# GpSimd's residuals wait for more of VectorE's instructions: the sign subtractions and the low parts of V

## The chip, the cores and the metric

The kernel runs on one core of a Trainium2 chip. Its time is the device time of one execution in microseconds (us). The profile names the engines PE (TensorE, matmuls), PEld (TensorE's loading of weights), DVE (VectorE), ACT (ScalarE), POOL (GpSimd) and SP (SyncE, which issues transfers).

## The reference

Two stages follow each other. The first is attention for 4 batches of 8 heads, 768 tokens, 64 columns, in which a query sees only the keys of its own hash bucket (the signs of six projections). The second lets each batch choose its 128 best tokens and adds a two-layer network's output to them.

```
mask = q_bucket[:, :, :, None] == k_bucket[:, :, None, :]
scores = np.where(mask, scale * q @ k.T, -1e9)
attn = softmax(scores);  x = attn @ v                       # float32, heads side by side
top = the 128 tokens of a batch with the largest x @ w_gate
out[top] = x[top] + sigmoid(score) * (relu(x[top] @ w1) @ w2)
```

## The kernel before, in words

Float32 values are carried as sums of two 16-bit parts, so that TensorE can work on 16-bit operands. For each of the 32 heads (h) the kernel

- places the head's queries, keys and hash signs as columns of a tile A (and low parts in B), by transfers from SyncE's queue;
- takes the row maxima of the masked scores (`max_unit`, L646, on TensorE; L654 on ScalarE; L663 on VectorE);
- computes the scores transposed, in nine units of 512 columns (`st_unit`, L697 and L701), and their exponentials P in float32 on ScalarE (`st_exp`, L715 and L717). P of a head comes in three tiles of two chunks each, P{h}_0 to P{h}_2;
- subtracts from P its upper 16 bits and so gets the residual R{h}_g of each tile (`r_chunk`): on VectorE one chunk at a time (L732), or on GpSimd both chunks at once (L735). `POOL_R` gives GpSimd tile 1 of the even heads and tiles 0 and 2 of the odd ones, none of the last head: 46 residuals;
- multiplies on TensorE (`av`, L760), per chunk and block of 128 queries, the upper half of P with V's high and low part, and R with V's high part, in this order. TensorE takes its matmuls in the order of the program.

V of a pair of heads is split into a high part by ScalarE (L550) and a low part by VectorE (`split_vl`, L556); for the last head the column of scores also has a low part (`score_vl`, L578). The signs of a group of four heads (two pairs) are made by `signs`: two comparisons on VectorE (L482) after the hash matmuls (L465), and, after the second half, the difference of the two halves of the keys' signs (L489; group 0's is on GpSimd). `k_diff` makes the same difference of the keys (L636). GpSimd also makes the low halves of the network's weights (`load_w`, L821), 16 subtractions.

The order of the work on all engines is written out by hand: ORDER is a list of event numbers, which the program issues one after the other; a negative number resumes a generator. One stretch of it (line 119) reads

```
45, 1300, 1208, 1277, 1153, 1043, 44, 46, -1, 1099, 1285, 1100, 1221, 1103, 1301, 1104, 1105,
```

where 44 and 46 are the two halves of `signs` for group 4, 1100 and 1103 are `r_chunk` of head 13 for the tiles 0 and 2 (R13_0 and R13_2, on GpSimd), 1104 and 1105 the first of head 13's products. A few numbers further on stands 1101, VectorE's residual R13_1.

Beside the waits for data, two helpers add waits by order. `mine(i)` notes a VectorE instruction as the latest one, and `turn(i)` makes a GpSimd subtraction wait until the VectorE instruction noted last is done. Before the change `mine` stands around L502 (low parts of queries and keys), L565, L636, L732 and L843 (comparisons for the ranks); `turn` stands around L735 and L821, 62 instructions.

Of the kernel before, what the change touches and what calls it, by code (L numbers as in the profile page):

```python
# [16 lines left out]
ALU = mybir.AluOpType  # L17
# [224 lines left out]
def body(ctx, tc, qk, v, pj, wg, w1, w2, cst, out):  # L242
    nc = tc.nc
# [113 lines left out]
    def mine(i):  # L357
        st["port"] = i
# [9 lines left out]
    def need(*keys):  # L368

        assert all(k in st for k in keys), keys  # L370
# [101 lines left out]
    def signs(g, e):  # L472
        hp = st["hp", g, e]
        if ("sg", g) not in st:
            st["sg", g] = sb.tile([P, S // 2 + S], F16, tag="sg", name=f"sg{g}", bufs=2)
        if g > 1:
            need(("ps", 4 * g - 4))
        for j in range(2):
            st["sgd", 2 * g + j, e] = True
        t = st["sg", g]  # L480
        sd, sg = t[:, : S // 2], t[:, S // 2 :]
        nc.vector.tensor_scalar(  # L482
            sg[:, e * 384 : (e + 1) * 384], hp[:, :384], pjt[:, 66:67], pjt[:, 67:68],
            op0=ALU.is_gt, op1=ALU.mult,
        )
        pmax.give(f"hp{g}_{e}")
        if e:
            eng = nc.vector if g else nc.gpsimd
            eng.tensor_tensor(sd, sg[:, 0:384], sg[:, 384:768], op=ALU.subtract)  # L489

    def split_xh(p, r):
        if ("T", p) not in st:
# [59 lines left out]
    def split_vl(pr):  # L552
        need(("vh", pr))
        st["vl", pr] = True
        t, vv = st["V", pr], V[pr % NV].rearrange("p c h d -> p (c h) d")
        nc.vector.scalar_tensor_tensor(  # L556
            vv[:, :, VL : VL + D], t.rearrange("p c h d -> p (c h) d"), VS, vv[:, :, :D],
            op0=ALU.mult, op1=ALU.subtract,
        )

    def score_v():
        need(("vh", NH // 2 - 1))
# [12 lines left out]

    def score_vl():
        need("gvh")
        nc.vector.scalar_tensor_tensor(  # L578
            V[VLAST][:, :, 1, VL + D + 1 : VL + OW], st["gv"], VS, V[VLAST][:, :, 1, D + 1 : OW],
            op0=ALU.mult, op1=ALU.subtract,  # L580
        )
        st["gvl"] = True

    def sum_v(g):
# [642 lines left out]
    for g in range(NH // 4):  # L1227
        for e in range(2):
            at(hash_half, g, e)
            at(signs, g, e)  # L1230
    for fn in (score_v, score_vh, score_vl):
        at(fn)
# [4 lines left out]
    for h in range(NH):  # L1237
# [15 lines left out]
        if h % 2 == 0:  # L1253
            for fn in (load_v, split_vh, split_vl):
                at(fn, h // 2)
            g, k = GROUP[h // 2]
            if k == len(SUMS[g]) - 1:
                for fn in (sum_v, sum_hi, sum_lo):
                    at(fn, g)
# [92 lines left out]
```

## Time and profile before

| | |
|---|---|
| median of 3 runs | 392.65 us (392.45 to 396.61) |
| the profiled execution's own time | 393.02 us |
| its span, first to last instruction | 391.2 us |
| busy: PE, PEld, DVE, ACT, POOL | 379.8, 276.0, 326.1, 333.4, 180.2 us |
| chain that ended last, share on PE | 81% |
| L735 on POOL, 46 instructions | 132.3 us busy, 2879 ns mean, 138.4 us idle before them |
| L556 on DVE, 16 instructions | 15.4 us busy, 961 ns mean |
| L489 on DVE, 7 instructions | 2.5 us busy, 358 ns mean |

Times of instructions count from the span's start. The difference of 1.8 us between the execution's time and its span lies outside of all instructions. A row of a timeline gives the start, the duration, engine, line and operation, what it writes and reads, and in brackets how long its engine had been idle before it, with what ended that.

### The profile page before, as it was taken

What the parts mean: (1) busy time and instruction counts of PE and PEld (TensorE: products, weight loads), DVE (VectorE), ACT (ScalarE), POOL (GpSimd) and SP (SyncE); (2) the same over time, 40 slices, a digit from 0 to 9 for tenths busy, and PEclk for the clock granted to TensorE, in tenths of its full rate; (3) what the DMA queues carried; (4) which work ended last, traced back from release to release, by engine and by line L of the source; (5) the groups of instructions that cost most, each with busy time, mean ns of one, the idle gap of its engine ahead of it and who ended that gap; (6) DMA issues with size and microseconds to landing.
All of it is one profiled execution on the core that took longest, in us unless ns stands there. A gap on an engine that the chain in (4) does not pass through costs nothing.

```text
span 391.2 us, 14365 instructions
## 1 busy us (share of the span) xinstructions
PE 379.8 (97%) x5768; PEld 276.0 (71%) x5768; DVE 326.1 (83%) x903; ACT 333.4 (85%) x817; POOL 180.2 (46%) x103
## 2 busy tenths in 40 slices
PE   7889999999999999999999999999999999999995
PEld 4247677677766777787757777677777778778794
DVE  4879888889899989888897889988998888689732
ACT  6989999999999999988879999989999897775310
POOL 6436676564647268652245343555335354500122
PEclk9999999999999999999999999999999999999999
DMA  8676676677566377375583536646654422000511
GB/s 266 151 198 193 168 235 180 198 218 209 147 189 179 95 186 208 103 211 144 144 238 104 131 85 165 160 112 153 195 155 111 94 55 66 22 22 2 175 45 54
DMA packets 26354, 56.38 MB, mean 144 GB/s; under 512 B 4218, under 2 KB 10942, under 8 KB 26288
## 3 DMA queue, kind: packets, MB, share of 16 engines
q1 hardware_dynamic: 15936, 36.92, 36.0%
q10 hardware_dynamic: 9680, 16.45, 13.2%
q0 software_dynamic: 672, 2.10, 1.7%
q8 instruction: 45, 0.74, 0.8%
q14 instruction: 21, 0.17, 0.1%
HBM read 26.58 MB, written 7.35 MB: 87 GB/s over the span
## 4 chain that ended last, share of the span: by engine, by line
PE 81%; ACT 7%; issue 4%; DMA 4%; POOL 1%; DVE 1%; SPq 1%; POOLq 0%; ACTq 0%
PE av L760 25%; PE st L697 14%; PE st L701 14%; PE bank L646 14%; PE bank L978 4%; PE bank L465 3%; PE bank L1002 3%; DMA A<-sg 2%; ACT me L654 2%; ACT P L715 2%; PE av L745 1%; ACT x L784 1%; DMA out_3l_dram<-x 1%; ACT P L717 1%; DMA Xa<-in_qk_dram 1%
## 5 line engine op out<-in xcount | busy, mean ns | idle before, releaser
L735 POOL TENSOR_TENSOR R<-P 128x1536 f16<-128x1536 f32 x46 | 132.3, 2879 | 138.4 <-ACT P L717 25.1
L760 PEld LDWEIGHTS <-P 128*128 128x128 bf16 x2304 | 125.5, 98 | 25.4 <-issue 1.1
L760 PE MATMUL av<-V,P 128*128 128x65 f16 (+2 forms) x2304 | 132.5, 193 | 0.0
L663 DVE CUSTOM_DVE_ANT_0 mj<-bank,me 128x384 bf16<-128x384 f32 x192 | 102.2, 552 | 29.6 <-ACT me L654 14.5
L760 PE MATMUL av<-V,R 128*128 128x65 f16 (+1 forms) x1152 | 125.8, 193 | 0.0
L715 ACT ACTIVATE P<-st 128x512 f32<-128x512 f32 x192 | 113.8, 613 | 10.4 <-PE st L701 4.3
L697 PE MATMUL st<-A 128*128 128x512 f16 (+1 forms) x384 | 119.1, 326 | 0.2
L701 PE MATMUL st<-B 128*128 128x512 f16 (+1 forms) x384 | 118.7, 325 | 0.0
L646 PE MATMUL bank<-A 128*128 128x384 f16 x384 | 107.5, 331 | 4.9 <-DMA A<-sg 2.7
L760 PEld LDWEIGHTS <-R 128*128 128x128 f16 x1152 | 105.8, 97 | 0.1
L654 ACT ACTIVATE me<-bank 128x384 f32<-128x384 f32 x192 | 94.3, 510 | 10.7 <-DVE M L663 4.8
L732 DVE TENSOR_TENSOR R<-P 128x768 f16<-128x768 f32 x100 | 94.9, 964 | 0.3 <-ACT P L717 0.2
L717 ACT ACTIVATE P<-st 128x512 f32<-128x512 f32 x96 | 58.8, 613 | 2.4 <-PE st L701 2.0
L646 PEld LDWEIGHTS <-A 128*128 128x128 f16 x384 | 35.3, 98 | 26.9 <-issue 6.8
L701 PEld LDWEIGHTS <-B 128*128 128x128 f16 x384 | 37.5, 98 | 15.4 <-issue 1.2
L697 PEld LDWEIGHTS <-A 128*128 128x128 f16 x384 | 37.5, 98 | 15.2 <-issue 2.5
L784 ACT ACTIVATE x<-av,rc 128x64 f32<-128x64 f32 x192 | 44.3, 334 | 0.4 <-DVE rc L772 0.4
L502 DVE SCALAR_TENSOR_TENSOR T<-X,T 128x768 f16<-128x768 f32 x32 | 30.9, 971 | 0.0
L495 ACT ACTIVATE T<-X 128x768 f16<-128x768 f32 x32 | 27.7, 867 | 0.0
L978 PEld LDWEIGHTS <-w1h 128*128 128x128 f16 x256 | 15.9, 98 | 2.6
L821 POOL TENSOR_TENSOR w1l<-W,w1h 128x512 bf16<-128x512 f32 x8 | 12.9, 1616 | 8.0 <-DVE R L732 7.8
L821 POOL TENSOR_TENSOR w2l<-W,w2h 128x512 bf16<-128x512 f32 x8 | 12.5, 1562 | 8.6 <-PE bank L646 3.7
(138 smaller groups left out, 405.0 us busy)
## 6 DMA issues: line engine op xcount, KB each, us to landing
X<-in_qk_dram SPq DMA_DIRECT2D x32, 384.0 KB
B<-T SPq DMA_DIRECT2D x62, 192.0 KB
A<-T SPq DMA_DIRECT2D x31, 240.0 KB
V<-in_v_dram ACTq DMA_DIRECT2D x16, 384.0 KB
out_dram<-x ACTq DMA_DIRECT2D x6, 768.0 KB
W<-in_w_dram ACTq DMA_DIRECT2D x8, 512.0 KB
sbc<-scores SPq DMA_DIRECT2D x3, 384.0 KB
A<-sg SPq DMA_DIRECT2D x31, 31.5 KB
```

What stands on the lines that cost most here:

```text
L646: nc.tensor.matmul(pt[:, :384], a[0][:, t * P : (t + 1) * P], a[1][:, 384:768] if i else K[h % NA], start=True, stop=True,)
L654: nc.scalar.activation(me, st["mx", h, t, 0][:, :384], AF.Relu)
L663: nc.vector.tensor_tensor_reduce(out=jk, in0=st["mx", h, t, 1][:, :384], in1=st["me", h, t], op0=ALU.add, op1=ALU.max, scale=1.0 / MS, sca ...
L697: nc.tensor.matmul(pt[:, o : o + n], a[1][:, c * P : (c + 1) * P], a[0][:, q0 : q0 + n], start=True, stop=False,)
L701: nc.tensor.matmul(pt[:, o : o + n], bt[:, 0, c * P : (c + 1) * P], bt[:, 1, q0 : q0 + n], start=False, stop=True,)
L715: nc.scalar.activation(pp[:, r, 0:512], pt, AF.Exp, scale=ES)
L717: nc.scalar.activation(pp[:, :, 512:768], pt.rearrange("p (a b) -> p a b", a=2), AF.Exp, scale=ES)
L732: mine(nc.vector.tensor_tensor(t[:, r], pp[:, r], hi_view(pp, r), op=ALU.subtract))
L735: turn(nc.gpsimd.tensor_tensor(t, pp, hi_view(pp, a), op=ALU.subtract))
L760: nc.tensor.matmul(o[:, t, :n], l, vv[:, c, hh, v0 : v0 + n], start=False, stop=last and l is lo, skip_group_check=True,)
L784: nc.scalar.activation(x[:, t], o[:, t, :D], AF.Copy, scale=rc[:, t : t + 1])
L978: nc.tensor.matmul(hp[:, f * P : (f + 1) * P], w[:, k, o : o + P], x[:, k * P : (k + 1) * P], start=(f == 0 and k == 0 and i == order[0]), ...
```

## The change

`mine` is put around three more groups of VectorE's instructions: the sign subtractions of groups 1 to 7 (L489), the 16 low parts of V (L556) and the low part of the scores' column (L578). A GpSimd subtraction that stands behind one of them in the program, with no other noted instruction between, then waits for it. ORDER, the instructions and their operands are the same.

```
         if e:
-            eng = nc.vector if g else nc.gpsimd
-            eng.tensor_tensor(sd, sg[:, 0:384], sg[:, 384:768], op=ALU.subtract)
+            if g:
+                mine(nc.vector.tensor_tensor(sd, sg[:, 0:384], sg[:, 384:768], op=ALU.subtract))
+            else:
+                nc.gpsimd.tensor_tensor(sd, sg[:, 0:384], sg[:, 384:768], op=ALU.subtract)
...
-        nc.vector.scalar_tensor_tensor(
+        mine(nc.vector.scalar_tensor_tensor(
             vv[:, :, VL : VL + D], t.rearrange("p c h d -> p (c h) d"), VS, vv[:, :, :D],
             op0=ALU.mult, op1=ALU.subtract,
-        )
+        ))
...
-        nc.vector.scalar_tensor_tensor(
+        mine(nc.vector.scalar_tensor_tensor(
             V[VLAST][:, :, 1, VL + D + 1 : VL + OW], st["gv"], VS, V[VLAST][:, :, 1, D + 1 : OW],
             op0=ALU.mult, op1=ALU.subtract,
-        )
+        ))
```

## Rows read from the trace of the kernel before

**Rows 1.** The page: busy time by engine; the chain that ended last, by engine.
```profile
PE 379.8 (97%) x5768; PEld 276.0 (71%) x5768; DVE 326.1 (83%) x903; ACT 333.4 (85%) x817; POOL 180.2 (46%) x103
...
PE 81%; ACT 7%; issue 4%; DMA 4%; POOL 1%; DVE 1%; SPq 1%; POOLq 0%; ACTq 0%
```

**Rows 2.** Stretches: length, each engine's busy time (instructions), granted clock, DMA share, GB/s.
```profile
core 0: us, PE busy (x) PEld busy (x) DVE busy (x) ACT busy (x) POOL busy (x), PEclk, DMA share, GB/s
162.00:166.00 4.00, 4.00 (x73) 3.43 (x72) 2.83 (x9) 3.88 (x9) 2.49 (x1) 1.00 0.29 66
161.30:366.50 205.20, 204.54 (x3266) 153.16 (x3265) 176.76 (x498) 175.74 (x434) 81.46 (x32) 1.00 0.44 117
```

**Rows 3.** TensorE's timeline: start us, duration, instruction, idle before it and releaser.
```profile
254.86 0.34 PE L646 MATMUL bank<-A 128*128 128x384 f16 x1 [0.62 <-DMA A<-sg]
```

**Rows 4.** Line 735: duration ns min/median/max, first and last start; who waited for it.
```profile
L735 POOL TENSOR_TENSOR R<-P x46: 2737/2747/3457, 25.5 to 337.5; 128x1536 f16<-128x1536 f32 x46
...
who waited for it (us, times):
  POOL R L735: 2.6, 2
```

**Rows 5.** VectorE's timeline around two GpSimd residuals that meet its instructions.
```profile
250.76 0.36 DVE L489 TENSOR_TENSOR sg<-sg 128x384 f16<-128x384 f16 x1
251.04 1.82 DVE L732 TENSOR_TENSOR R<-P 128x768 f16<-128x768 f32 x2
...
253.96 0.56 DVE L663 CUSTOM_DVE_ANT_0 mj<-bank,me 128x384 bf16<-128x384 f32 x1 [0.62 <-ACT me L654]
...
278.60 0.95 DVE L732 TENSOR_TENSOR R<-P 128x768 f16<-128x768 f32 x1
279.47 0.94 DVE L556 SCALAR_TENSOR_TENSOR V<-V,V 128x768 f16<-128x768 f32 x1
```

**Rows 6.** GpSimd's timeline: R13_0, R13_2, R21_0, R21_2 and R24_1.
```profile
157.79 2.75 POOL L735 TENSOR_TENSOR R<-P 128x1536 f16<-128x1536 f32 x1 [1.84 <-ACT me L654]
161.41 3.08 POOL L735 TENSOR_TENSOR R<-P 128x1536 f16<-128x1536 f32 x1 [0.88 <-POOL R L735]
...
247.44 3.30 POOL L735 TENSOR_TENSOR R<-P 128x1536 f16<-128x1536 f32 x1 [7.32 <-PE st L701]
252.16 3.30 POOL L735 TENSOR_TENSOR R<-P 128x1536 f16<-128x1536 f32 x1 [1.42 <-ACT me L654]
...
279.71 3.30 POOL L735 TENSOR_TENSOR R<-P 128x1536 f16<-128x1536 f32 x1 [5.71 <-DVE R L732]
```

**Rows 7.** TensorE's timeline: the first matmuls with R13_0, R13_2 and R24_1.
```profile
161.30 0.19 PE L760 MATMUL av<-V,R 128*128 128x65 f16 x1
...
165.16 0.19 PE L760 MATMUL av<-V,R 128*128 128x65 f16 x1
...
283.83 0.19 PE L760 MATMUL av<-V,R 128*128 128x65 f16 x1
```

**Rows 8.** Line 556: duration ns min/median/max, first and last start us.
```profile
L556 DVE SCALAR_TENSOR_TENSOR V<-V,V x16: 944/952/1096, 16.1 to 328.4; 128x768 f16<-128x768 f32 x16
```

**Rows 9.** VectorE's timeline at the first key difference and around group 4's signs.
```profile
8.46 0.36 DVE L424 TENSOR_TENSOR A<-A 128x384 f16<-128x384 f16 x1
...
157.26 0.35 DVE L636 TENSOR_TENSOR T<-T 128x384 f16<-128x384 f16 x1
...
159.35 1.27 DVE L482 TENSOR_SCALAR sg<-bank,pjt 128x384 f16<-128x384 f32 x2
160.66 0.36 DVE L489 TENSOR_TENSOR sg<-sg 128x384 f16<-128x384 f16 x1
160.93 0.95 DVE L732 TENSOR_TENSOR R<-P 128x768 f16<-128x768 f32 x1
```

**Rows 10.** TensorE's timeline at the start.
```profile
6.32 1.04 PE L309 MATMUL wq<-ones 128*128 128x128 f16 x8
8.87 1.54 PE L646 MATMUL bank<-A 128*128 128x384 f16 x4 [1.51 <-DVE A L424]
...
16.76 0.61 PE L309 MATMUL wq<-ones 128*128 128x128 f16 x8
...
20.37 0.65 PE L646 MATMUL bank<-A 128*128 128x384 f16 x3 [2.04 <-DMA A<-sg]
```

## The prediction

> **What bounds the kernel now.** I read the engine totals first, then the chain of waits, then stretches, then the timelines of single engines. TensorE is busy for 379.8 of 391.2 us and the chain that ends last lies on it for 81% [rows 1]. Between 161.3 and 366.5 us it is idle for only 205.20 - 204.54 = 0.66 us [rows 2], nearly all of it one wait of 0.62 us for a transfer of signs at 254.86 [rows 3]. So whatever holds TensorE up before 366.5 has almost nothing to disappear in: it reaches the end of the program nearly whole. GpSimd is busy for 46% and VectorE for 83%. Later work on either costs nothing unless TensorE has to wait for it. In the profile nobody but GpSimd itself waits for a residual of line 735 [rows 4]; every one is ready when TensorE asks. The question is which of them the new waits make late.
>
> **Which waits move.** `turn` makes a GpSimd subtraction (46 residuals, 16 low halves of weights) wait for the last VectorE instruction that went through `mine`. An added `mine` changes such a wait only if it stands, in the order of the program, between the last old `mine` and that `turn`. I walked through ORDER and paired the k-th call of a line with its k-th row. Of 62 waits 13 move: nine residuals and one weight half to a low part of V (line 556), R30_1 to the low part of the scores' column (line 578), and R13_0 and R13_2 to the sign subtraction of group 4. The other 49 name the same instruction as before.
>
> **The eleven waits for low parts.** R24_1 shows the pattern. The old wait, for VectorE's residual (278.60 + 0.95 = 279.55), lets GpSimd start at 279.71 [rows 5, 6], 0.16 us later. By then the low part of V runs, 279.47 to 280.41, and GpSimd's subtraction takes 3.30 us in place of the usual median of 2.747 [rows 4 to 6]: it ends 283.01 - 280.41 = 2.60 us after the VectorE instruction that it met. The same holds at 252.16, behind two VectorE residuals that end at 252.86: 255.46 - 252.86 = 2.60 [rows 5, 6]. So these two engines already keep out of each other's way; a GpSimd subtraction that comes too early is held until VectorE is through. With the new wait it starts at 280.41 + 0.16 = 280.57 and ends 2.75 later, at 283.32: 0.31 us **later** than now, though its row becomes shorter by 0.55. The other ten lose between nothing (where the exponentials set the start anyway) and the same 0.31. TensorE first needs R24_1 at 283.83 [rows 7], 0.82 us after its present end; that is the narrowest margin of the eleven, so none reaches TensorE. Cost: 0. What is behind it: VectorE's next subtraction that needs the same way in can be pushed by up to 0.31. At 250.76 the sign subtraction of group 6 starts just behind R21_0 (247.44 + 3.30 = 250.74) [rows 5, 6] and would move to about 251.05. VectorE's next idle time, 0.62 us ahead of the maximum at 253.96 [rows 5], takes that up; if it had none there, I count up to 0.31 at three such places, 0.9 in all, as the upper bound, and nothing as the lower one. A gain for VectorE I bound by nothing: its low parts of V take 944 to 1096 ns with a median of 952 [rows 8], so hardly any is being stretched now.
>
> **The two waits for the sign subtraction.** Here the distance is large. R13_0 now starts at 157.79, behind the key difference of line 636 (157.26 + 0.35), and ends at 160.54 [rows 6, 9]. Between that difference and the sign subtraction of group 4 VectorE works through a maximum, three small operations of the reciprocal, another maximum and two sign comparisons; the subtraction runs from 160.66 to 161.02 [rows 9]. None of these waits for R13_0, so they stay where they are. R13_0 can then start at 161.02 + 0.16 = 161.18 instead of 157.79. But VectorE goes straight on to its own residual, 160.93 to 161.88 [rows 9], and holds GpSimd up as above: R13_0 ends at 161.88 + 2.60 = 164.48, **3.94 us later** than now. TensorE's first matmul with R13_0 is the third of head 13's products, at 161.30 [rows 7]. It runs in order, so everything behind stands still: 164.48 - 161.30 = 3.18, and the handoff. The trace of before has no wait of TensorE for GpSimd. The nearest rows are its start behind VectorE's first key difference, which ends at 8.46 + 0.36 = 8.82 and lets TensorE start at 8.87 [rows 9, 10], and the 0.16 from VectorE to GpSimd. I take 0.1 us, nearer the first, since the waiting engine is the same, and bound it by 0.05 from below and 0.3, twice the second, from above. The stall is 3.3 us, with bounds of 3.2 and 3.5; if R13_0 met no VectorE instruction it would end at 161.18 + 2.75 = 163.93 and the stall would be 2.7.
>
> **Behind R13_0** stand on GpSimd R13_2 and two weight halves. R13_2 follows at once, 164.48 to 167.23; TensorE asks for it at 165.16 now [rows 7], by then some 3.3 us later, at about 168.5, so it costs nothing more. The weight halves are first read long after. No transfer is issued from GpSimd's queue near here. VectorE's next maxima need TensorE's matmuls behind the stall, so they move with it, as ScalarE's exponentials do.
>
> **The sum.** Eleven waits 0, R13_0 +3.3, R13_2 0; TensorE's later 0.66 us of idle time [rows 2] could take back at most that; the transfer behind most of it is issued long after 161, by a queue that also waits for TensorE's work, so I take off nothing and keep 0.66 for the lower bound. The profiled execution took 393.02 us (span 391.2), 0.1% over the median of 392.65; on it that makes 396.3, on the median **395.95**. With the bounds, 2.7 - 0.7 = 2.0 to 3.5 + 0.9 = 4.4, this case alone covers 394.6 to 397.1.
>
> **Rivals.**
> 1. **TensorE's clock falls in the stall, and the kernel is slower by more than 1%.** The granted clock is 1.00 in these stretches [rows 2], and an idle time of 2.04 us at 18.34 left the rate as it was: three matmuls of line 646 in 0.65 us right behind it, against 1.54 for four at 8.87, when TensorE still ran at half rate [rows 10]. A pause of 3.3 us does not occur once it is warm. For it: the pause is 1.6 times the longest that is shown. Against: TensorE is busy without a gap before and after. Price: at the start eight 128-column matmuls take 1.04 us at 6.32 and 0.61 at 16.76 [rows 10], so from 8.87 to about 16.1, some 7.2 us, it ran at half rate; as long a stretch here loses 3.6 us, a short one 1.5. Sum 3.3 + 1.5 to 3.6: 397.5 to 399.6 us. It decides from the point where the pause is long enough for the 2.4 GHz level to be withdrawn, which no row shows. The Trainium skill, "TensorE: Matmul & The Clock Gate", Part 1, says that the throttled state is the default and activity releases it; by that rule this pause could cost as rival 1 says, and the trace so far shows only that 2.04 us is too short. Chance 0.13.
> 2. **The delay is taken back or is smaller.** R13_0 might start before VectorE's residual takes hold (stall 2.7), the engines that run ahead in the stall might spare TensorE its small waits (0.66), and the matmul records could hide more slack. Price +0.5 to +2.0: 393.2 to 394.6. Against it stands TensorE's full row from 162 to 166 [rows 2] and up to 366.5. Chance 0.14.
> 3. **The wait isn't there.** If the order of calls didn't put group 4's signs ahead of R13_0, only the waits for V would move: 392.7. But ORDER has 44 and 46 (the signs) ahead of 1100 (R13_0) on one line, and the trace has line 489 beginning right after R13_0's present end and ahead of VectorE's residual. Chance 0.03.
>
> **How the numbers follow.** The forecast holds with 0.66, and 0.04 is left for what I don't foresee; 395.95 is the forecast's time. For 8 in 10 I reach down into rival 2 and up to the lower end of rival 1: 393.8 to 398.0. What a measurement here can tell from no change is about 1%, 3.9 us. Slower by more than that: rival 1's 0.13, the forecast's upper end (over 396.6) 0.10, half of the unforeseen 0.02. Faster by over 1% would need 3.9 us taken from TensorE, whose work is unchanged: the other 0.02. The rest, 0.73, lies within 1%.
>
> **What would show it.** R13_0 starts at about 161.2 and ends near 164.5; TensorE shows a wait of some 3.3 us at line 760 ended by GpSimd's line 735, where before there was none; rows of TensorE before 161 keep their times, and those after are late by a constant to the end. Residuals of line 735 lose their 3.30 us rows where they met line 556. A granted clock below 1.00 after 161 would mean rival 1; a stall with no difference in the span, rival 2; line 735 at 157.8 as now, rival 3.

## The result

The change makes the kernel slower: 398.11 us (median of 14 runs, 397.03 to 400.82) against 393.44 for before in the same runs (median of 14, 392.45 to 396.61), a ratio of 1.0116 with a 95% interval of 1.0089 to 1.0143. Two later series with the same kernel gave 1.0142 [1.0104, 1.018] and 1.0107 [1.0065, 1.0148]. A ratio is estimated from the runs of its series and is not exactly the quotient of the two medians shown beside it. The forecast was +3.3 us (1.0084), 395.95, with a range up to 398.0. The profiled execution of after took 397.33 us, 4.31 over that of before.

In after.py the lines behind 490 have numbers higher by two: L762 is `av`, L737 GpSimd's residual, L734 VectorE's, L558 the low part of V. The page of after, busy time by engine and the chain by engine, beside [rows 1]:

```profile
PE 380.3 (96%) x5758; PEld 276.9 (70%) x5768; DVE 327.3 (83%) x903; ACT 334.0 (84%) x817; POOL 179.2 (45%) x103
...
PE 75%; ACT 9%; issue 5%; DVE 4%; DMA 4%; POOL 2%; POOLq 0%; SPq 0%; ACTq 0%; DVEq 0%
```

The work is the same (ten of TensorE's 5768 matmul records are missing from this trace), the span 4.4 us longer. TensorE's waits in after, longest first (total us, times, longest), have one that [rows 4] did not know:

```profile
PE av L762 <- POOL R L737: 3.1, 1, 3.1
PE bank L648 <- DMA A<-sg: 2.1, 1, 2.1
PE bank L648 <- DVE A L424: 1.5, 1, 1.5
```

Its place, in three timelines of after (start us, duration, instruction): VectorE's signs of group 4 and its residual R13_1, GpSimd's R13_0, and TensorE's first products of head 13, which answer to [rows 6, 7, 9]:

```profile
161.50 0.36 DVE L489 TENSOR_TENSOR sg<-sg 128x384 f16<-128x384 f16 x1
161.78 0.95 DVE L734 TENSOR_TENSOR R<-P 128x768 f16<-128x768 f32 x1
```
```profile
162.03 3.31 POOL L737 TENSOR_TENSOR R<-P 128x1536 f16<-128x1536 f32 x1 [5.45 <-PE bank L648]
```
```profile
162.11 0.22 PE L762 MATMUL av<-V,P 128*128 128x65 f16 x2
165.39 0.20 PE L762 MATMUL av<-V,R 128*128 128x65 f16 x1 [3.06 <-POOL R L737]
```

The sign subtraction ends at 161.86, R13_0 starts 0.17 later, meets R13_1 (to 162.73), ends 2.61 after it at 165.34, and TensorE goes on 0.05 later. (The bracket names "PE bank L648", which had long been done; that the wait is for the signs is shown below, where R13_0 is moved ahead of them.)

Where the other microsecond comes from is seen by comparing the k-th weight load of TensorE in two traces (there are 5768 in each): the difference of their start times is how late TensorE is by then. Its steps, by the time in before's first trace, in us:

```
                          63.3   109.0  122.3  161.4  161.8-163.6   163.1    rest   end
after                     +0.19  +0.08  +0.27  +3.29     0            -      0.48  +4.31
after_again               +0.21  +0.14  +0.27  +3.39   +1.51          -      1.86  +7.38
after_third               +0.16  +0.13  +0.28  +3.28   +1.63          -      2.80  +8.28
before_again                0      0      0      0       -          +1.08    3.94  +5.02
```

"Rest" holds steps that also come without the change: at the start, at 79 to 84, at the hash matmuls near 158, near 260 and 365. They vary from one execution to the next by more than 2 us, so single executions can't be compared by their ends, only by their steps. Three steps belong to the change (63, 122 and 161), and a small one at 109.0, where TensorE waits 0.16 us for VectorE's maximum in after. The columns at 161.8 and 163.1 hold two losses that I had not put into the sum: one right behind the stall in two of the three profiles of the change, and one at 163.1 in an execution of **before**.

### The profile page after: what moved, and what is told of

The parts are those of the page before. It is cut to its first block, busy times and chain, and to the rows that moved or that the text cites. A ratio compares the mean times of both kernels' runs of the same rounds, so it can differ in the third digit from the quotient of the medians.

```text
span 395.6 us, 14355 instructions
## 1 busy us (share of the span) xinstructions
PE 380.3 (96%) x5758; PEld 276.9 (70%) x5768; DVE 327.3 (83%) x903; ACT 334.0 (84%) x817; POOL 179.2 (45%) x103
## 4 chain that ended last, share of the span: by engine, by line
PE 75%; ACT 9%; issue 5%; DVE 4%; DMA 4%; POOL 2%; POOLq 0%; SPq 0%; ACTq 0%; DVEq 0%
PE av L762 23%; PE bank L648 13%; PE st L699 13%; PE st L703 13%; PE bank L980 4%; PE bank L465 3%; ACT me L656 2%; PE bank L1004 2%; ACT P L717 2%; ACT x L786 1%; ACT P L719 1%; PE av L747 1%; DVE R L734 1%; DVE mj L665 1%; DMA out_3l_dram<-x 1%
## 5 line engine op out<-in xcount | busy, mean ns | idle before, releaser
L737 POOL TENSOR_TENSOR R<-P 128x1536 f16<-128x1536 f32 x46 | 131.1, 2852 | 143.8 <-DVE V L558 24.6
L762 PEld LDWEIGHTS <-P 128*128 128x128 bf16 x2304 | 125.5, 98 | 25.6 <-issue 1.3
L762 PE MATMUL av<-V,P 128*128 128x65 f16 (+2 forms) x2304 | 132.8, 193 | 0.1
L762 PE MATMUL av<-V,R 128*128 128x65 f16 (+1 forms) x1152 | 125.8, 193 | 3.1 <-POOL R L737 3.1
L699 PE MATMUL st<-A 128*128 128x512 f16 (+1 forms) x384 | 119.1, 326 | 0.2
L648 PE MATMUL bank<-A 128*128 128x384 f16 x384 | 107.5, 331 | 5.2 <-DMA A<-sg 2.1
L762 PEld LDWEIGHTS <-R 128*128 128x128 f16 x1152 | 105.8, 97 | 3.4 <-POOL R L737 3.2
L734 DVE TENSOR_TENSOR R<-P 128x768 f16<-128x768 f32 x100 | 96.0, 975 | 0.4 <-ACT P L719 0.2
L648 PEld LDWEIGHTS <-A 128*128 128x128 f16 x384 | 35.2, 98 | 26.8 <-issue 6.7
L699 PEld LDWEIGHTS <-A 128*128 128x128 f16 x384 | 37.5, 98 | 15.5 <-issue 2.8
```

The source lines that it names most:

```text
L648: nc.tensor.matmul(pt[:, :384], a[0][:, t * P : (t + 1) * P], a[1][:, 384:768] if i else K[h % NA], start=True, stop=True,)
L699: nc.tensor.matmul(pt[:, o : o + n], a[1][:, c * P : (c + 1) * P], a[0][:, q0 : q0 + n], start=True, stop=False,)
L734: mine(nc.vector.tensor_tensor(t[:, r], pp[:, r], hi_view(pp, r), op=ALU.subtract))
L737: turn(nc.gpsimd.tensor_tensor(t, pp, hi_view(pp, a), op=ALU.subtract))
L762: nc.tensor.matmul(o[:, t, :n], l, vv[:, c, hh, v0 : v0 + n], start=False, stop=last and l is lo, skip_group_check=True,)
```

## The experiments

**The parts alone.** The signs alone:

```
-            eng = nc.vector if g else nc.gpsimd
-            eng.tensor_tensor(sd, sg[:, 0:384], sg[:, 384:768], op=ALU.subtract)
+            if g:
+                mine(nc.vector.tensor_tensor(sd, sg[:, 0:384], sg[:, 384:768], op=ALU.subtract))
+            else: ...
```

> Only the sign subtractions are noted; the low parts of V are not. Theory A (the stall at R13_0 passes whole to the end, the waits for low parts add the rest): R13_0 starts near 161.2 and ends near 164.5, one TensorE wait of 3.0 to 3.2 us at line 760, time +3.2 to +3.6 us over the kernel before (ratio 1.008 to 1.009). Rival B (the low parts' waits cost nothing, and what the stall costs beyond its length is given away behind it): the same stall, but +4.2 to +4.7 us (ratio 1.011 to 1.012). Rival C (the stall is absorbed and the low parts' waits are the cost): under +1.5 us.

Measured: 399.05 us against 395.27 (23 runs), ratio 1.0117 [1.0074, 1.016]; a wait of 3.1 us at L762, a step of 3.50 at 161.4, none at 63.3, 109.0 and 122.3, and 1.14 more behind the stall. The whole of the stall comes from the signs, and it alone costs as much as I had given to the whole change, or more: over the +3.2 to +3.6 us of theory A. The ratio is rival B's, and one half of rival B is right: something is lost behind the stall, where the granted clock is 0.50 from 165.1 to 168.4 (more of it below). Its other half, that the low parts cost nothing, the next runs answer.

The low parts alone, the signs as before:

```
-        nc.vector.scalar_tensor_tensor(...)          # L556, L578
+        mine(nc.vector.scalar_tensor_tensor(...))
```

> Only the low parts of V and of the scores' column are noted; the sign subtractions are not. Theory A: no TensorE wait for GpSimd near 161; steps of about 0.2 near 63 (behind R3_0 and R3_2) and 0.3 near 122 (behind R9_0), time +0.4 to +0.9 us (ratio 1.001 to 1.002). Rival B: 0 (ratio 0.999 to 1.001). Rival C: +3 us or more.

Measured: 396.17 against 395.27, ratio 1.0006 [0.9976, 1.0036]. No TensorE wait for GpSimd, steps of 0.13 at 109.0 and 0.28 at 122.3. The step near 63 that theory A gave is missing (0.04): between 59 and 61 TensorE had fallen 0.14 us further behind in this execution. The size that theory A gave, 0.1 to 0.2%, is within the interval, and so is nothing at all; the steps decide, not the time.

**The order.** The whole change, with R13_0 issued ahead of the signs, so that it doesn't wait for them:

```
-    45, 1300, 1208, 1277, 1153, 1043, 44, 46, -1, 1099, 1285, 1100, 1221, ...
+    45, 1300, 1208, 1277, 1153, 1043, 1100, 44, 46, -1, 1099, 1285, 1221, ...
```

> The whole change, but GpSimd's R13_0 is issued, in the order of the program, ahead of group 4's signs, so that it waits for the key difference as before; every engine keeps its order. R13_2 still waits for the signs. Theory A: the stall at 161 is gone, the time is that of the low parts alone, +0.4 to +0.9 us. Rival B: 0. Rival C: the time of the change, +4 us or more.

Measured: 394.82 against 395.27, ratio 1.0012 [0.9983, 1.004]. The stall is gone with the one moved number; steps of 0.19 at 63.3, 0.13 at 109.0 and 0.27 at 122.3 are left. So the 3.3 us hang on R13_0's wait for the signs alone and not on R13_2's, which still waits for the signs here.

**The change and before once more**, with no edit.

> The change once more, to see which of the steps between its trace and that of before come back. Theory A: stall of 3.2 us at line 762, steps of 0.2 near 63 and 0.3 near 122 again, while the small ones (0.1 at the start, 0.07 near 110, 0.2 at 159 to 161, 0.13 near 366) need not; time +4.0 to +4.9 us (ratio 1.010 to 1.0125). Rival B: only the stall comes back, and the rest of the 4.3 us sits behind it at other places.

Measured: 400.48 against 395.27, ratio 1.0142 [1.0104, 1.018]; the steps stand in the table and come back as theory A has it, but the time is 5.2 us over before, more than its +4.9. Behind the stall, the granted clock falls. Stretches (from:to, length, busy time of PE, PEld, DVE, ACT, POOL, granted clock, DMA share, GB/s) of after_again and, with no fall, of after:

```profile
166.80:170.10 3.30, 3.30 (x33) 2.25 (x30) 0.00 (x0) 0.60 (x1) 2.46 (x1) 0.50 0.05 10
170.60:180.00 9.40, 9.40 (x155) 7.67 (x152) 7.73 (x22) 7.76 (x18) 3.19 (x3) 1.00 0.68 180
```
```profile
165.40:168.80 3.40, 3.40 (x59) 2.88 (x60) 1.25 (x5) 1.18 (x3) 2.64 (x1) 1.00 0.07 16
```

At 0.50 TensorE gets 33 matmuls done in 3.3 us, against 59 in 3.4 us, and the 128x512 matmul of L699 takes 0.62 us there (PE timeline of after_again, first row) in place of 0.38 (that of after, second row):

```profile
167.37 0.62 PE L699 MATMUL st<-A 128*128 128x512 f16 x1
```
```profile
165.88 0.38 PE L699 MATMUL st<-A 128*128 128x512 f16 x1
```

> The kernel before, once more, as a control for single profiles. If small steps of 0.1 to 0.2 us between two profiles are noise, this one differs from the first profile by up to 0.3 us in all, with such steps at the start, at the hash matmuls (line 465) and near 366, and with none at 63 and 122. If they belong to the change, it is the same everywhere to 0.05 us.

Measured: 398.07 us, one execution. No steps at 63 and 122, as expected, but 5.02 us in all in place of up to 0.3, and a step of 1.08 at 163.1 that was not expected at all. GpSimd's and VectorE's timelines of this execution, and TensorE's waits from 160 to 170:

```profile
160.10 2.75 POOL L735 TENSOR_TENSOR R<-P 128x1536 f16<-128x1536 f32 x1 [1.84 <-ACT me L654]
163.73 2.75 POOL L735 TENSOR_TENSOR R<-P 128x1536 f16<-128x1536 f32 x1 [0.88 <-POOL R L735]
```
```profile
164.37 2.32 DVE L489 TENSOR_TENSOR sg<-sg 128x384 f16<-128x384 f16 x1
166.61 0.95 DVE L732 TENSOR_TENSOR R<-P 128x768 f16<-128x768 f32 x1
167.48 0.47 DVE L617 SCALAR_TENSOR_TENSOR W<-WH,cs,bank 128x260 f16<-128x260 f16 x1
```
```profile
PE bank L646 <- DVE W L617: 0.9, 1, 0.9
PE bank L465 <- DMA X<-in_qk_dram: 0.6, 1, 0.6
```

The sign subtraction of group 4, 0.36 us in [rows 9], takes 2.32 here: TensorE waited 0.6 us for a load at the hash matmuls, the signs came late with them, R13_2 started first and held VectorE until it was through (163.73 + 2.75 = 166.48). So before runs a race between these two instructions. Its first trace shows it won, 160.66 against 161.41. The Trainium skill, "SBUF — State Buffer", section "SBUF: two separate sides", says that VectorE and GpSimd share a pair of ports as an exclusive lock: of a VectorE instruction with two inputs in SBUF and a GpSimd one that reads SBUF, whichever starts first keeps it for its whole instruction. Both of the subtractions here read both of their inputs from SBUF; the 2.32 and, the other way round, the 2.61 us above agree.

**Who is held.** The whole change, but R13_1 (event 1101) behind W's low part (1302) on VectorE, so that R13_0 meets nothing:

```
-    1090, 1101, 1157, 1279, 1154, 1107, 1223, 1222, 1278, 1302, 1343, ...
+    1090, 1157, 1279, 1154, 1107, 1223, 1222, 1278, 1302, 1101, 1343, ...
```

> The whole change, but VectorE makes its own residual R13_1 behind W's low part, not right behind the sign subtraction, so that GpSimd's R13_0 meets nothing when it is released. Theory A (GpSimd is held by the VectorE instruction that it meets): R13_0's row takes 2.75 us and not 3.31, the TensorE wait is 2.5 to 2.7 us and not 3.1, and R13_1 is now the one that is held, until R13_0's end + 0.8. Rival (the longer row has another cause): 3.3 us again.

Measured: R13_0's row takes 2.75 us (162.86 to 165.61) and TensorE's wait at L762 is 2.50 us. R13_1 is now the one that is held, until 0.81 behind R13_0's end (VectorE's timeline):

```profile
162.33 0.36 DVE L489 TENSOR_TENSOR sg<-sg 128x384 f16<-128x384 f16 x1
162.89 0.49 DVE L619 SCALAR_TENSOR_TENSOR W<-WH,cs,bank 128x260 f16<-128x260 f16 x1 [0.20 <-ACT WH L609]
163.29 3.13 DVE L734 TENSOR_TENSOR R<-P 128x768 f16<-128x768 f32 x1
```

As theory A has it, 0.56 of the 3.06 us come from meeting R13_1. The clock fell behind this shorter pause too (0.50 from 166.6 to 169.9). The times of this execution, 399.19, and of the next two, 394.41 and 395.96, are single ones and decide nothing; their steps do.

**The low parts of two pairs, each alone** (3 in the first kernel, 6 in the second):

```
-        nc.vector.scalar_tensor_tensor(...)          # L556
+        i = nc.vector.scalar_tensor_tensor(...)
+        if pr in (3,):
+            mine(i)
```

> Of the change only the wait for the low part of V of pair 3 (R3_0 waits for it). Theory A: R3_0 ends 0.3 us later, VectorE's R3_1 and its low part of the keys behind it too, GpSimd's R3_2 with them, and TensorE is 0.15 to 0.2 us later from 63.4 on; no other step. Rival B: no step at 63.

Measured: a step of 0.17 at 63.3, none at 109.0 and 122.3. GpSimd's R3_0 and R3_2, in this execution and then in before's:

```profile
56.38 2.75 POOL L737 TENSOR_TENSOR R<-P 128x1536 f16<-128x1536 f32 x1 [1.25 <-ACT me L656]
60.11 3.31 POOL L737 TENSOR_TENSOR R<-P 128x1536 f16<-128x1536 f32 x1 [0.98 <-ACT P L719]
```
```profile
55.60 3.31 POOL L735 TENSOR_TENSOR R<-P 128x1536 f16<-128x1536 f32 x1 [0.39 <-DVE T L636]
60.20 3.00 POOL L735 TENSOR_TENSOR R<-P 128x1536 f16<-128x1536 f32 x1 [1.29 <-ACT P L717]
```

R3_0 (first row) ends at 59.13 in place of 58.91; TensorE being 0.08 us ahead of before's trace here, that is 0.3 us later. VectorE's R3_1 and then its low part L502 of the next pair are held that much longer, R3_2 meets the latter and takes 3.31 us in place of 3.00. Measured from TensorE's work R3_2 ends 0.3 us later too, and TensorE loses 0.17 of that, so it had little more than 0.1 us to spare for R3_2 before.

> Of the change only the wait for the low part of V of pair 6 (R9_0 and a weight half wait for it). Theory A: R9_0 ends 0.3 us later, VectorE's R9_1 and all behind it up to the maxima near 122 too, and TensorE waits 0.2 to 0.3 us for a bank there; no other step. Rival B: no step at 122.

Measured: a step of 0.27 at 122.3 and none at 63.3 or 109.0. VectorE's R9_1 is held 0.26 us longer behind R9_0 (its row in before, then here), all behind it is late, and TensorE waits for a maximum (PE timeline):

```profile
118.01 1.22 DVE L732 TENSOR_TENSOR R<-P 128x768 f16<-128x768 f32 x1
```
```profile
118.16 1.48 DVE L734 TENSOR_TENSOR R<-P 128x768 f16<-128x768 f32 x1
```
```profile
122.68 0.32 PE L648 MATMUL bank<-A 128*128 128x384 f16 x1 [0.20 <-DVE M L665]
```

In this execution, too, R13_2 came first at 162, by 0.02 us, the sign subtraction took 2.94 us, and TensorE waited 1.48 us for W, which VectorE makes behind it (GpSimd's, VectorE's and TensorE's timelines):

```profile
161.83 2.75 POOL L737 TENSOR_TENSOR R<-P 128x1536 f16<-128x1536 f32 x1 [0.88 <-POOL R L737]
```
```profile
161.85 2.94 DVE L489 TENSOR_TENSOR sg<-sg 128x384 f16<-128x384 f16 x1
```
```profile
166.11 0.32 PE L648 MATMUL bank<-A 128*128 128x384 f16 x1 [1.48 <-DVE W L619]
```

**The race taken out, without the stall**: the signs alone are noted, and R13_0 stands ahead of them.

> Only the sign subtractions are noted, and R13_0 is issued ahead of group 4's signs, so that R13_2 alone waits for them. Theory D (before has a race: where VectorE's sign subtraction of group 4 comes a little late, R13_2 gets in first and holds it for 2 us or more, and TensorE loses 1.1 to 1.7 us): the row of line 489 at 161 takes 358 ns in every profile, no stall, no steps at 63 and 122, and the time is that of before less the share of its executions that lose the race, -0.3 to -1.0 us (ratio 0.9975 to 0.999), with fewer executions in the upper group. Rival E (the long row of line 489 is a chance of a few profiles and no part of the spread): ratio 1.000, the same two groups of times.

Measured: 394.28 us (12 runs, 393.12 to 396.14) against 394.43 (23 runs, 392.47 to 397.04), ratio 0.9989 [0.9961, 1.0017]. The profile has L489 at 357 to 359 ns for all groups, no stall and no steps at 63 to 122. Over 395 us lie 3 of 12 runs, against 10 of 23 of before. This is the way theory D says, but the interval holds 1.000, so a gain is not shown and rival E isn't out.

**The clock.** The whole change with dead matmuls where TensorE would wait (they add five lines, so `av` is L767 here):

```
+            if h == 13:
+                for _ in range(56):
+                    nc.tensor.matmul(o[:, NC * OW : 508], ones16, ones16[:, : 508 - NC * OW], ...)
```

> The whole change, with 56 idle matmuls of 112 columns into spare columns, issued on TensorE just ahead of head 13's products, where it would wait for R13_0 anyway. They add dead work and change no output. Theory F (in part of the executions the stall makes TensorE's clock fall to half for 3.4 us, which costs 1.5 us more): granted clock 1.00 behind the stall, TensorE's idle time at line 762 under 0.6 us, and the time 0.5 to 1.5 us under that of the change in the same set of runs. Rival G (the clock's fall is an accident of those profiles): the same time as the change, within 0.3 us, or longer by the part of the idle matmuls that does not fit.

> The change a third time, beside the kernel with idle matmuls. Theory F: the stall of 3.2 us again, and behind it with a chance of about three in four a stretch of 3.4 us at half the clock; time +4.0 to +5.2 us. Rival G: no such stretch, +3.9 us.

Measured, in one series: 397.33 with the dead matmuls (12 runs, 395.54 to 399.46), ratio 1.008 [1.0054, 1.0107]; the change itself 399.29 (6 runs, 397.17 to 401.3), ratio 1.0107. TensorE's timeline with the dead matmuls, and stretches of it and of after_third behind the wait:

```profile
163.34 2.92 PE L748 MATMUL av<-ones 128*128 128x112 f16 x56
166.79 0.20 PE L767 MATMUL av<-V,R 128*128 128x65 f16 x1 [0.30 <-POOL R L737]
```
```profile
167.00:170.00 3.00, 3.00 (x56) 2.48 (x53) 1.05 (x5) 0.99 (x3) 2.44 (x1) 1.00 0.07 14
```
```profile
167.20:170.50 3.30, 3.30 (x27) 2.04 (x24) 0.42 (x1) 0.60 (x1) 2.04 (x1) 0.50 0.08 16
```

The delay is the same, the pause is not, and the clock holds in the profile. As it held in one profile of the change as well, the times have to speak: the medians are 1.96 us apart, by the ratios it is 1.1 us, and the intervals of the ratios overlap, so the size is loose; theory F's 0.5 to 1.5 holds the second and not the first. The profiles say more on the cause: behind a pause of 2.5 to 3.1 us at this place the clock fell in four of five, and in none of the eight without such a pause (before, before_again, e2_vlow, e3_order, e5_pair3, e6_pair6, e8_first and e9_heat) did it fall there. The ratio with the clock held, 1.008, is nearly the forecast's 1.0084, but in part by luck: the low parts' loss and the gain from the race, both left out of the forecast, almost cancel in it.

**What the waits by order are worth at all**: before without them.

```
-TURNS = True
+TURNS = False
```

> The kernel before without any wait by order (no GpSimd subtraction waits for VectorE). Theory D (the waits decide who goes first; whoever comes second is held): GpSimd starts as soon as the exponentials are there, VectorE's rows of lines 732, 502 and 556 grow to 2 to 3.5 us in many places, and the time is longer by 2 us or more. Rival H (the engines keep out of each other's way without them, so the waits only cost): the time is shorter by 0.5 to 3 us.

Measured: 434.23 us (6 runs), ratio 1.0991 [1.0939, 1.1042]. VectorE's residuals there (ns min/median/max), where before's longest is 1411, and TensorE's longest waits, which before did not have at this size:

```profile
L732 DVE TENSOR_TENSOR R<-P x100: 915/953/3499, 29.7 to 400.7; 128x768 f16<-128x768 f32 x100
```
```profile
PE bank L646 <- DVE M L663: 17.2, 15, 4.2
PE av L760 <- DVE R L732: 5.3, 5, 2.0
```

Rival H is out: the waits are worth some 40 us. VectorE's busy time grows from 326.1 to 368.4 us. Theory D's long rows are there, but few: 5 of 100 residuals, 3 of 32 low parts of queries and keys and 1 of 16 low parts of V are over 1.6 us; the rest of the growth is spread over other lines. TensorE, which needs VectorE's maxima, idles 41 us in place of 11 (span less busy time), and its busy time is 12 us longer, the granted clock being 0.50 in four stretches of about 17 us together.

## Why the prediction was wrong

**Where the number fell.** The increase was 4.7 us (398.11 - 393.44) and not 3.3. The range was missed by 0.11 us, and that is also the base's doing: before's median in these 14 runs lies 0.79 over the 392.65 of three runs that the forecast started from. On that base 4.7 us would have ended inside the range, by its width and not by its sum.

**Right, step by step.** Which waits move; that R13_0's decides; its start 0.17 us behind the signs (0.16 forecast); the 2.60 us behind the VectorE instruction that it meets (2.61); the handoff to TensorE (0.05, the lower bound; 0.1 taken); the stall (3.28 to 3.39 us in the three profiles of the change, 3.3 forecast; the 3.50 of the signs alone has some of the slow clock in it). R13_2 cost nothing more. Nothing was taken back: TensorE is 4.10 us late at 163 and 4.18 at 363 in after.

**Wrong: "a chance of 0.13" for rival 1.** I gave the fall of TensorE's clock a small chance and left it out of the sum, because 2.04 us of idle time had not brought it [rows 10]. It came in four of the five profiles with such a pause: after_again, after_third and the signs alone (3.06 us) and e4_nohold (2.50), not in after (3.06). It cost 1.5 to 1.6 us in after_again, after_third and e4_nohold; in the signs alone, where it began inside the pause, 1.1 us and a part of the 3.50. That is the lower end of rival 1's price, and so luck: no row stood behind its 1.5, and the 3.6 that was worked out from rows did not come. One quiet pause of 2.04 us was no evidence that 3 us would be quiet as well. With the low parts alone, the clock was at 0.50 right behind the pause at the start, 2.32 us in that execution (its PE timeline and a stretch):

```profile
20.97 1.12 PE L646 MATMUL bank<-A 128*128 128x384 f16 x3 [2.32 <-DMA A<-sg]
```
```profile
20.60:23.80 3.20, 2.83 (x10) 1.38 (x11) 0.76 (x3) 1.92 (x4) 0.00 (x0) 0.50 0.81 174
```

Pauses of 2.31 and 2.37 us at the same place left it at 1.00 in before_again and e5_pair3. So the length of a pause alone does not tell whether the clock falls, and why it held in after the runs do not show. The Trainium skill, "TensorE: Matmul & The Clock Gate", Part 1, says that the throttled state is the default and activity releases it; I had weighed that as a rival, and the four falls agree with it.

**Wrong: "so none reaches TensorE. Cost: 0"**, of the eleven waits. They cost 0.16 to 0.21 + 0.08 to 0.14 + 0.27 us at 63.3, 109.0 and 122.3, about 0.6 in sum. I looked at the margin of each residual whose wait moved, and TensorE waited for none of these. What was late was the next in line: R3_2, whose own wait had not moved but which meets a VectorE instruction that R3_0 had pushed, and the maxima behind R9_1. The pushes of 0.3 us I had named, with 0.9 as their bound, and set at nothing in the sum. Pairs 3 and 6 are shown each alone; which wait makes the step at 109.0 was not separated.

**Missing: what the change gives back.** The traces of before and of the kernels without the sign wait lose the race of R13_2 against the sign subtraction in three of five profiles (before_again, e2_vlow and e6_pair6; not before and e5_pair3), and 1.1 to 1.7 us with it. The change ends this race, since R13_2 then stands behind R13_0 and the signs. I had one trace of before, in which it was won by 0.75 us, and took it for the rule; in e5_pair3 it was won by 0.29.

An estimate from these: 3.3 + 0.6 + 4/5 of 1.5, less 3/5 of 1.4, gives 4.3 us; the three series say 4.2 to 5.6 by their ratios, 4.7 to 5.2 by their medians. The shares come from five profiles each and are rough. Whether the version without the race (e8_first) is faster than before, by about 0.1%, stays open.

## What to carry to other kernels

When an order-only wait is made stricter, look for the instruction whose new releaser is furthest away in time, and sum its wait against the margin of its first user on the bounding engine; then go one instruction further on each engine behind the late one. A pause of TensorE can cost more than its length, here by about 1.5 us at half the clock in four of five profiles, and filling it with dead matmuls helps to tell the two apart. Before costing a wait by one trace, ask by how little the order in that trace was decided.

## What the runs showed that was not expected

- Two instructions 0.02 us apart (161.83 and 161.85) decided about 1.6 us of TensorE's time: GpSimd's subtraction, once it had started, held VectorE's to its end, and a subtraction of 0.36 us took 2.3 to 2.9 us.
- The waits by order in this kernel are worth 10% of its time, though each is a wait; without them TensorE's clock fell four times too.
- Single executions of one kernel differ by up to 5 us, so steps between traces tell more than their ends.
